# Attention beside the first product by whole tiles of 128 tokens, with another decoding order and another end

## The chip, the cores and the metric

The kernel runs on one core of one Trainium2 chip. The metric is the device time of one execution in microseconds. Three runs of the kernel before took 1620.76, 1622.3 and 1623.78 us; the median is 1622.3.

## The reference

Attention over chunks of 64 tokens (8 batches, 8 heads, 576 tokens, 64 wide), then two dense blocks over 4608 tokens (512 to 2048 to 512), the first with a squared relu, the second with a smooth step:

```python
def _attn_ref(q, k, v):            # all cut into chunks of 64 tokens
    scores = (1 / sqrt(D)) * matmul(q_c, k_c^T)
    scores = scores - max(scores)
    attn = exp(scores); attn = attn / (sum(attn) + 1e-09)
    return matmul(attn, v_c)

x = attn_out.transpose(0, 2, 1, 3).reshape(B * S, H * D)     # 4608 x 512
h = x @ w_in;  x = (maximum(h, 0) ** 2) @ w_out
h = x @ w_in2; g = where(h >= 1, h, where(h <= -1, 0, (h + 1) ** 2 / 4)); out = g @ w_out2
```

The weights arrive as float64 and are decoded on the chip.

## The kernel before, in words

**Stages.** `plain_h` forms x @ w_in in 9 blocks of 512 tokens; it is the first stage, with attention and all the decoding beside it. Three more stages (`form_b`, `form_a`, `form_b` again) form the other three products with seven half-size products each (P1 to P7) in the manner of Strassen; the change touches of these only the last stores.

**Products.** An operand is held as a high and a low part (xh, xl for x; ih, il for w_in), and each product is three matmuls: high by high, low weight by high, high weight by low.

**Slots.** All instructions are written out by hand in the order of a list of slots. Slot 2 (16 j + fi) + c of the first stage is half c of the product for block j and weight piece fi: six matmuls of 512 columns into `ph`. After the second half, ACT takes the relu (`g`), POOL squares it, and SP issues the store to DRAM. `ph` has two banks, so the relu of a piece must be done before the product after the next begins. Slots 0 to 287 are the first stage (SB1 = 288). `at_slot(s, fn)` puts a helper behind the six matmuls of slot s; what was registered first comes first. Each engine, and SP with its DMA issues, works through its own part of this order strictly in sequence; a slot fixes the order, not the time.

**Attention.** A tile is 128 tokens, a unit four heads of a tile (UT = 2 units a tile, 72 units). A unit goes through: `att_a` (four transposes of q and k into psA), `att_ae` (ACT copies them to qkT), `att_b` (psB, the scores, and DVE's maximum m), `att_exp` (ACT, four exponentials with their sums z), `att_n` (DVE adds 1e-9 and takes the reciprocal, POOL scales s), `att_c` (two transposes into psC), `att_ce` (ACT to atT), `att_d` (psD, the product with v), `att_x` (ACT xh, DVE xl). `head(i)` runs this for the first tiles ahead of the loop, one unit a step. In the loop `turn(i)` takes four slots (PER = 4) and holds the parts of four units: slot 0 of a turn psD of the unit three back, psB and its maximum of the unit one back, and xh, xl; slot 1 the exponentials; slot 2 psC, atT and the normalising of the unit behind; slot 3 psA, qkT and the loads of later tiles.

**Decoding of w_in.** `stage_piece` loads a piece (two buffers `ws`), `piece_a` takes its absolute value on ACT and runs three bit operations on DVE (tile `wy`), `piece_b` one more on DVE and then ACT's copy to ih, `piece_c` subtracts on POOL (il). `decode()` runs c, b and a of three neighbouring pieces; six decodes stand in the head (DEC), the others are spread over the first slots (PACE), each ahead of its slot's attention.

**Decoding of the other weights.** 48 units (`unit_a` to `unit_d`: DVE, POOL sums, ACT, DVE, stores) start at slot U0 = 22, one every UPER = 5.1 slots; `stage_unit` of the first two stands three slots ahead.

**The end.** In the last stage P4's tiles of the last token pair are copied by ACT from PSUM, transposed by DVE (`store`) and stored with four DMAs each, all issued by SP.

Of the kernel before, what the change touches and what calls it, by code (L numbers as in the profile page):

```python
# [8 lines left out]
F32 = mybir.dt.float32  # L9
# [22 lines left out]
def chunk_attention_moe_moe2(ctx, tc, q, k, v, w_in1, w_out1, w_in2, w_out2, out):  # L32
# [91 lines left out]
    def wy():  # L124
        n_y[0] += 1
        return rt(4 + n_y[0] % 3, [P, 4 * P], "wy", U32)
# [123 lines left out]
    att = {}  # L250
# [45 lines left out]
    def att_ae(u):  # L296
        qkT = ep.tile([P, 2, NP, P], F32, tag="qkT", name="qkT", bufs=2)
        nc.scalar.activation(out=qkT[:, 0], in_=att[u][:, 0], func=AF.Copy, scale=SCALE)
        nc.scalar.copy(qkT[:, 1], att[u][:, 1])
        att[u] = qkT  # L300

    def att_b(u):

        qkT = att[u]
        pt = pa.tile([P, 2, 512], F32, tag="qk", name="psB")
        for p in range(NP):
# [9 lines left out]
        sc = pt[:, :, 0:2 * CH].rearrange("q e (c k) -> q e c k", c=2)  # L316
        m = ep.tile([P, 2, 2], F32, tag="m", name="m", bufs=3)
        z = ep.tile([P, 2, 2], F32, tag="z", name="z", bufs=3)
        nc.vector.tensor_reduce(out=m, in_=sc, op=ALU.max, axis=AX.X, negate=True)
        att[u] = [sc, m, z]  # L320

    def att_exp(u):
        sc, m, z = att[u]
        s = ep.tile([P, 2, 2, CH], F32, tag="s", name="s", bufs=2)
        for e in range(2):
            for c in range(2):
# [7 lines left out]
        att[u] = [s, z]  # L334

    def att_n(u):
        s, z = att[u]
        nc.vector.tensor_scalar_add(z, z, 1e-9)
        nc.vector.reciprocal(z, z)
        s4 = s.rearrange("q e c k -> q (e c) k")  # L340
        z4 = z.rearrange("q e c -> q (e c)")
        nc.gpsimd.tensor_tensor(out=s4, in0=s4, in1=z4.unsqueeze(2).to_broadcast([P, HU, CH]), op=ALU.mult)

    def att_c(u):
        s, _ = att[u]
        pt = pa.tile([P, 2, NP, CH], F32, tag="t", name="psC", padded_shape=[P, HU, 2, CH], bufs=2)
        for e in range(2):
            nc.tensor.transpose(  # L348
                pt[:, e].rearrange("k p t -> k (p t)"), s[:, e].rearrange("q c k -> q (c k)"), ident
            )  # L350
        att[u] = pt

    def att_ce(u):
        at = ep.tile([P, 2, NP, CH], F32, tag="atT", name="atT", bufs=2)
        nc.scalar.copy(at, att[u])
        att[u] = at

    def att_d(u):

        at = att[u]  # L360
        pt = pa.tile([P, 2, 512], F32, tag="d", name="psD")
        for p in range(NP):
            for c in range(2):
                for e in range(2):
                    nc.tensor.matmul(  # L365
                        pt[rows(e), c, p * CH:(p + 1) * CH],
# [5 lines left out]
        att[u] = pt  # L372

    def att_x(u):
        pt = att.pop(u)
        (xh, xl), a, n = unit_x(u)[0]
        o = pt[:, :, 0:NP * CH].rearrange("d c (p t) -> d p c t", p=NP)
        xh, xl = (x.rearrange("d p (c t) -> d p c t", c=2) for x in (xh, xl))
        nc.scalar.copy(xh, o)
        nc.vector.tensor_tensor(out=xl, in0=o, in1=f(xh), op=ALU.subtract)  # L380
# [16 lines left out]
    RG = tuple(range(7, 13))  # L397
# [167 lines left out]
    def form_b(w, j, prod, kk):  # L565
# [20 lines left out]
        for dp in range(2):  # L586
            c = c_tile(n)
            if key is None:
# [11 lines left out]
    def store(j, dh, th, dp, c):  # L600
# [5 lines left out]
        for a in range(P // G):  # L606
            nc.sync.dma_start(
# [10 lines left out]
    LB, LC, LD, LV = 1, 2, 3, 0  # L618
    PER = 4
    DEC = (1, 2, 4, 6, 8, 10)  # L620
    PACE = 0.78
    U0, UPER = 22, 5.1
# [28 lines left out]
    with tc.manual_schedule():  # L651
# [14 lines left out]
        strokes = []  # L666
        for p in range(NF):
            strokes.append([(piece_a, p), (piece_b, p), (piece_c, p)])
# [14 lines left out]
        def turn(i):  # L683

            res = [[] for _ in range(4)]

            def put(n, fn, u):
                if 0 <= u < NU:
                    res[n].append((fn, (u,)))

            put(0, att_d, i - LD)
            put(0, att_b, i - LB)
            put(0, att_x, i - LD)
            put(1, att_exp, i - LB)
            put(2, att_c, i - LC)
            put(2, att_ce, i - LC)
            put(2, att_n, i - LB)
            put(3, att_a, i)
            put(3, att_ae, i)
            if i >= LV and (i - LV) % UT == 0 and i - LV < NU:  # L700
                res[3].append((load_v, ((i - LV) // UT,)))
            if i % UT == UT - 1 and i // UT + QB < NU // UT:
                res[3].append((load_qk, (i // UT + QB,)))
            return res

# [4 lines left out]
        n0 = tiles_until(0) * UT  # L710
        def head(i):
            def do(fn, u, hi=NU):
                if 0 <= u < hi:
                    fn(u)

            do(att_b, i - LB)
            do(att_x, i - LD - 1)
# [4 lines left out]
            do(att_ae, i)  # L722
            do(att_ce, i - LC)
            if i in DEC:
                decode()
            do(att_n, i - LB)
            if (i - LV) % UT == 0:
                load_v((i - LV) // UT)
            if i % UT == UT - 1:
                load_qk(i // UT + QB)  # L730

        for i in range(n0 + LD):
            head(i)
        att_x(n0 - 1)
        for i in range(n0 + LD, NU + LD):
            g = int((i - n0 - LD) * PER)
            for c, group in enumerate(turn(i)):
                for fn, args in group:
                    at_slot(g + c, fn, *args)

        for j in range(1, NBL):
            assert int((tiles_until(j) * UT - 1 - n0) * PER) < 2 * NF * j, j
        done = int((NU + LD - 1 - n0 - LD) * PER) + 4

# [110 lines left out]
        for s in range(END + 40):  # L855
# [3 lines left out]
            if n_dec[0] < NF + 2 and n_dec[0] < len(DEC) + 1 + PACE * ((s + 2) // 2):  # L859
                decode()  # L860
# [6 lines left out]
        assert not todo and not pe and not wst and n_dec[0] == NF + 2  # L867
# [32 lines left out]
```

## Time and profile before

| | |
|---|---|
| median of three runs | 1622.3 us |
| profiled execution | 1622.09 us, its span 1620.3 us |
| mean granted TensorE clock | 0.994 |
| TensorE busy | 1586.6 us (98%) |
| DVE, ACT, POOL busy | 1089.7, 868.5, 413.3 us (67, 54, 26%) |

The span runs from the first to the last instruction; what the measured time holds beyond it lies around the program. An engine's busy share is over the whole span; stages differ, so the windows further down say more. A wait in brackets is idle time just before that group of instructions, and the name behind the arrow is what ended it.

### The profile page before, as it was taken

How to read it: one execution, taken by the hardware profiler on the slowest of the kernel's cores; microseconds unless marked ns; L12 is line 12 of the kernel's file. 1: busy time of each engine (PE TensorE's matmuls, PEld its weight loads, DVE VectorE, ACT ScalarE, POOL GpSimd, SP SyncE). 2: the span in 40 equal slices, each digit the busy share in tenths (PEclk: the TensorE clock that was granted, in tenths of full speed). 3: DMA queues.
4: the chain of work that ended last, by engine and by line, in shares of the span. 5: the costliest groups of instructions: out<-in, count | busy, mean ns of one | idle time of the engine just before them, and what ended most of it. 6: DMA issues, size and time to landing. Idle time of an engine off the chain costs nothing.

```text
span 1620.3 us, 27342 instructions
## 1 busy us (share of the span) xinstructions
PE 1586.6 (98%) x9504; PEld 1362.6 (84%) x9504; DVE 1089.7 (67%) x1437; ACT 868.5 (54%) x1852; POOL 413.3 (26%) x461
## 2 busy tenths in 40 slices
PE   7889999999999999999999999999999999999998
PEld 5667777777778899999888898898888899998887
DVE  5956666665443376777677666857574787877786
ACT  7656666666553344344444566666665434444442
POOL 2657666665444200000000333333220000000000
PEclk9999999999999999999999999999999999999999
DMA  9769999999996982625378665574679773563723
GB/s 213 204 185 295 291 290 287 293 302 281 277 301 205 318 250 91 216 62 190 110 219 254 210 230 178 190 238 159 240 244 337 248 199 99 129 170 83 207 37 49
DMA packets 442730, 339.47 MB, mean 210 GB/s; under 512 B 214240, under 2 KB 419040, under 8 KB 442592
## 3 DMA queue, kind: packets, MB, share of 16 engines
q1 hardware_dynamic: 442592, 337.73, 69.3%
q8 instruction: 75, 1.23, 0.3%
q14 instruction: 63, 0.52, 0.1%
HBM read 195.04 MB, written 142.61 MB: 208 GB/s over the span
## 4 chain that ended last, share of the span: by engine, by line
PE 87%; DVE 5%; ACT 2%; DMA 2%; issue 2%; POOL 1%; SPq 0%; DVEq 0%; ACTq 0%; POOLq 0%
PE X L451 34%; PE ph L409 23%; PE V L451 17%; PE W L451 8%; PE psA L291 1%; PE psD L365 1%; PE psB L309 1%; DVE ol L441 1%; DVE t L532 1%; PE psC L348 1%; DMA ws<-in_moe_w_in_dram 1%; ACT s L327 1%; DVE wy L115 1%; DVE xr L445 0%; DVE wy L118 0%
## 5 line engine op out<-in xcount | busy, mean ns | idle before, releaser
L451 PE MATMUL X<-oh,w 128*128 128x448 f32 (+1 forms) x1920 | 557.5, 371 | 1.5 <-DVE c L512 1.5
L440 ACT CAST oh<-gr 128x896 fp32r<-128x896 f32 (+1 forms) x280 | 270.0, 964 | 334.1 <-PE X L451 160.5
L441 DVE TENSOR_TENSOR ol<-gr,oh 128x896 fp32r<-128x896 f32 (+1 forms) x280 | 314.5, 1124 | 182.6 <-ACT oh L440 175.3
L451 PEld LDWEIGHTS X<-oh,w 128*128 128x128 f32 x1920 | 360.0, 188 | 43.8 <-DVE c L512 1.9
L451 PE MATMUL X<-ol,w 128*128 128x448 f32 (+1 forms) x960 | 356.4, 371 | 4.2 <-DVE ol L441 4.2
L451 PE MATMUL V<-oh,w 128*128 128x448 f32 (+1 forms) x960 | 278.5, 371 | 0.0
L409 PE MATMUL ph<-xh,ih 128*128 128x512 f32 x576 | 245.3, 426 | 0.0
L409 PE MATMUL ph<-xl,ih 128*128 128x512 f32 x576 | 227.9, 396 | 0.0
L409 PE MATMUL ph<-xh,il 128*128 128x512 f32 x576 | 227.8, 395 | 0.0
L422 POOL TENSOR_TENSOR g<-g 128x512 f32<-128x512 f32 x144 | 171.3, 1189 | 143.6 <-ACT g L421 140.5
L451 PEld LDWEIGHTS X<-ol,w 128*128 128x128 f32 x960 | 180.1, 188 | 26.7 <-DVE ol L441 6.3
L451 PEld LDWEIGHTS V<-oh,w 128*128 128x128 f32 x960 | 180.2, 188 | 20.9
L445 DVE TENSOR_TENSOR gr<-gr,gr 128x896 f32<-128x896 f32 (+1 forms) x160 | 177.9, 1112 | 3.7 <-DMA gr<-g 3.7
L451 PE MATMUL V<-ol,w 128*128 128x448 f32 (+1 forms) x480 | 178.0, 371 | 0.0
L421 ACT ACTIVATE g<-ph 128x512 f32<-128x512 f32 x144 | 86.4, 600 | 134.8 <-PE ph L409 123.3
L451 PE MATMUL W<-oh,w 128*128 128x448 f32 (+1 forms) x480 | 139.4, 371 | 0.0
L409 PEld LDWEIGHTS ph<-xl,ih 128*128 128x128 f32 x576 | 109.3, 190 | 24.7
L409 PEld LDWEIGHTS ph<-xh,ih 128*128 128x128 f32 x576 | 109.4, 190 | 21.6
L409 PEld LDWEIGHTS ph<-xh,il 128*128 128x128 f32 x576 | 110.0, 191 | 16.6
L526 ACT ACTIVATE t<-c,half 128x448 f32<-128x448 f32 (+1 forms) x120 | 81.3, 681 | 70.9 <-DVE c L512 70.8
L441 POOL TENSOR_TENSOR ol<-xr,oh 128x896 fp32r<-128x896 f32 (+1 forms) x10 | 23.7, 2374 | 360.7 <-ACT oh L440 353.0
L532 DVE SCALAR_TENSOR_TENSOR t<-c,t 128x448 f32<-128x448 f32 (+1 forms) x120 | 96.4, 830 | 18.4 <-ACT t L526 18.2
(69 smaller groups left out, 1906.0 us busy)
## 6 DMA issues: line engine op xcount, KB each, us to landing
w<-w SPq DMA_DIRECT2D x168, 256.0 KB, 5.1
gr<-g SPq DMA_DIRECT2D x96, 448.0 KB, 5.2
gr<-g SPq DMA_DIRECT2D x64, 480.0 KB, 4.6
g<-t SPq DMA_DIRECT2D x96, 224.0 KB, 2.7
wu<-in_moe_w_out_dram SPq DMA_DIRECT2D x64, 256.0 KB, 4.6
g<-t SPq DMA_DIRECT2D x64, 240.0 KB, 4.4
w<-wh SPq DMA_DIRECT2D x32, 448.0 KB, 4.1
w<-wl SPq DMA_DIRECT2D x32, 448.0 KB, 5.0
```

The lines of the kernel that those rows point to most:

```text
L115: nc.vector.scalar_tensor_tensor(out=y, in0=w1, scalar=0xC0000000, in1=y, op0=ALU.bitwise_and, op1=ALU.bitwise_or)
L291: nc.tensor.transpose(pt[:, i, p, :], qkn[i][:, h0 + 2 * p:h0 + 2 * p + 2, :].rearrange("p h d -> p (h d)"), ident)
L309: nc.tensor.matmul(pt[rows(p), e, c * CH:(c + 1) * CH], qkT[rows(e), 0, p, rows(c)], qkT[rows(e), 1, p, rows(c)], start=True, stop=True,)
L409: nc.tensor.matmul(ph, win[fi][wi][:, kt * P:(kt + 1) * P], x[:, i, :], start=(kt == 0 and a == 0), stop=(kt == KT - 1 and a == 2),)
L421: nc.scalar.activation(out=g, in_=ph, func=AF.Relu)
L422: nc.gpsimd.tensor_tensor(out=g, in0=g, in1=g, op=ALU.mult)
L440: nc.scalar.copy(hi, raw)
L441: eng.tensor_tensor(out=lo, in0=raw, in1=f(hi), op=ALU.subtract)
L445: eng.tensor_tensor(out=o, in0=x, in1=z, op=ALU.subtract)
L451: nc.tensor.matmul(o, wt_[:, wi, c, :], x[:, i, :], start=first and a == 0, stop=last and a == 2, skip_group_check=True,)
L526: nc.scalar.activation(out=t, in_=h, func=AF.Square, bias=half, scale=0.5)
L532: nc.vector.scalar_tensor_tensor(out=t, in0=h, scalar=1.0, in1=t, op0=ALU.max, op1=ALU.min)
```

## The change

- A tile's two units are taken together in the loop: `tile_a` (eight transposes into two psA tiles), `tile_ae`, `tile_b`, `tile_exp` (once for each half e), `tile_n`, `tile_c`, `tile_ce`, `tile_d`, `tile_x`. A tile takes eight slots (PER = 8), g being the slot of its psB: psA at g - 4, psB, maximum and half of the exponentials at g (with psD and x of the tile before), the other half at g + 1, normalising at g + 4, psC and atT at g + 6, psD and x at g + 8. The first loop tile (4) has its psA, psB and exponentials in the head. qkT, s and atT hold a whole tile; qkT and atT have one buffer, s two.
- Of the decoding, ACT's copy to ih becomes a helper of its own (`piece_h`), run one decode later than `piece_b`; `piece_c` follows one later still; `wy` has four buffers and `g` five instead of six. A decode stands behind its slot's attention. The head holds seven (1, 2, 3, 5, 7, 9, 10), PACE is 0.8.
- U0 = 28 and UPER = 5 for the other weights.
- At the end P4's tiles of the last pair go from PSUM to DVE's transpose without ACT's copy, and of the last pair's first half of tokens (P2 and P4) every second store is issued by ACT.

```diff
-        return rt(4 + n_y[0] % 3, [P, 4 * P], "wy", U32)
+        return rt(4 + n_y[0] % 4, [P, 4 * P], "wy", U32)
...
+    def piece_h(p):
+        y, hi, lo = wst[p]
         nc.scalar.copy(hi, f(y))
...
+    def tile_a(t):
+        att[t, "a"] = []
+        for i in range(2):
+            pt = pa.tile([P, UT, NP, P], F32, tag="t", name="psA", bufs=2)
+            for h in range(0, H, 2):
+                nc.tensor.transpose(
+                    pt[:, h // HU, h // 2 % NP, :], qks[t][i][:, h:h + 2, :].rearrange("p h d -> p (h d)"), ident
+                )
+            att[t, "a"].append(pt)
+
+    def tile_ae(t):
+        q_, k_ = att.pop((t, "a"))
+        qkT = qkT_of(t * UT)
+        nc.scalar.activation(out=qkT[:, :, 0], in_=q_, func=AF.Copy, scale=SCALE)
+        nc.scalar.copy(qkT[:, :, 1], k_)
...
+    def normalize(s, z):
         nc.vector.tensor_scalar_add(z, z, 1e-9)
         nc.vector.reciprocal(z, z)
+        nc.gpsimd.tensor_tensor(out=s, in0=s, in1=z.unsqueeze(3).to_broadcast(list(s.shape)), op=ALU.mult)
...
+    def tile_b(t):
+        pt = pa.tile([P, 2, 512], F32, tag="qk", name="psB")
+        for i in range(UT):
+            scores(pt[:, :, i * 2 * CH:(i + 1) * 2 * CH], qkT_of(t * UT)[:, i])
+        att[t, "b"] = maxima(pt, UT * 2)
+
+    def tile_exp(t, e):
+        exps(s_of(t * UT), *att[t, "b"], (e,), UT * 2)
+
+    def tile_n(t):
+        normalize(s_of(t * UT), att.pop((t, "b"))[2])
...
+    def tile_c(t):
+        att[t, "c"] = pt = pa.tile([P, UT, 2, NP, CH], F32, tag="t", name="psC", bufs=2)
+        for i in range(UT):
+            turned(pt[:, i], s_of(t * UT), i)
+
+    def tile_ce(t):
+        nc.scalar.copy(at_of(t * UT), att.pop((t, "c")))
...
+    def tile_d(t):
+        att[t, "d"] = pt = pa.tile([P, 2, 512], F32, tag="d", name="psD")
+        for i in range(UT):
+            weigh(pt, t * UT + i, i * NP * CH)
+
+    def tile_x(t):
+        pt = att.pop((t, "d"))
+        for i in range(UT):
+            x_parts(pt, t * UT + i, i * NP * CH)
...
-    RG = tuple(range(7, 13))
+    RG = tuple(range(8, 13))
...
+            if key is None and w == 1 and j == NPAIR - 1:
+                store(j, dh, th, dp, o[dp])
+                continue
...
-            nc.sync.dma_start(
+            (nc.scalar if j == NPAIR - 1 and th == 0 and a % 2 else nc.sync).dma_start(
...
-    PER = 4
-    DEC = (1, 2, 4, 6, 8, 10)
-    PACE = 0.78
-    U0, UPER = 22, 5.1
+    PER, PH = 8, 4
+    DEC = (1, 2, 3, 5, 7, 9, 10)
+    PACE = 0.8
+    U0, UPER = 28, 5
...
-            if 0 <= n - 2 < NF:
-                piece_c(n - 2)
-            if 0 <= n - 1 < NF:
-                piece_b(n - 1)
+            for d, fn in ((3, piece_c), (2, piece_h), (1, piece_b)):
+                if 0 <= n - d < NF:
+                    fn(n - d)
...
+            if i == n0:
+                tile_a(T0_)
...
+            if i == n0 + 1:
+                for e in range(2):
+                    tile_exp(T0_, e)
...
+        for t in range(T0_, NTI):
+            g = PER * (t - T0_ - 1) + PH
+            if t > T0_:
+                at_slot(g - 4, tile_a, t)
+                at_slot(g - 4, tile_ae, t)
+                at_slot(g - 4, load_v, t)
+                if t + QB < NTI:
+                    at_slot(g - 4, load_qk, t + QB)
+                at_slot(g, tile_b, t)
+                at_slot(g, tile_x, t - 1)
+                at_slot(g, tile_exp, t, 0)
+                at_slot(g + 1, tile_exp, t, 1)
+                at_slot(g + 4, tile_n, t)
+            at_slot(g + 6, tile_c, t)
+            at_slot(g + 6, tile_ce, t)
+            at_slot(g + PER, tile_d, t)
+        at_slot(g + PER, tile_x, t)
...
-            if n_dec[0] < NF + 2 and n_dec[0] < len(DEC) + 1 + PACE * ((s + 2) // 2):
-                decode()
             i = 0
             while i < len(todo.get(s, ())):
...
             todo.pop(s, None)
+            if n_dec[0] < NF + 3 and n_dec[0] < len(DEC) + 1 + PACE * ((s + 2) // 2):
+                decode()
```

## Rows read from the trace of the kernel before

**Rows 1.** The page, part 4: the chain that ended last, by engine.
```profile
PE 87%; DVE 5%; ACT 2%; DMA 2%; issue 2%; POOL 1%; SPq 0%; DVEq 0%; ACTq 0%; POOLq 0%
```
**Rows 2.** Windows: start:end us, length, busy us (instructions) by engine, PEclk, DMA share, GB/s.
```profile
24.00:40.00 16.00, 14.23 (x174) 10.27 (x173) 11.65 (x29) 14.02 (x64) 5.41 (x7) 1.00 0.98 197
40.00:84.00 44.00, 39.87 (x314) 30.97 (x313) 40.93 (x58) 26.08 (x79) 29.01 (x23) 0.92 0.72 203
52.00:60.00 8.00, 6.96 (x48) 5.51 (x49) 7.56 (x12) 5.31 (x18) 5.70 (x5) 0.57 0.55 171
130.00:494.00 364.00, 364.00 (x3193) 288.68 (x3183) 217.69 (x396) 229.46 (x791) 215.60 (x271) 1.00 0.96 291
```
**Rows 3.** Windows of tile wy alone: length, busy DVE, ACT, POOL, then as above.
```profile
40.00:84.00 44.00, 35.64 (x37) 5.81 (x10) 15.04 (x9) 0.92 0.72 203
24.00:40.00 16.00, 7.55 (x12) 1.81 (x3) 3.05 (x3) 1.00 0.98 197
```
**Rows 4.** Timeline of TensorE, one steady turn: start us, us, instruction [idle before].
```profile
304.42 0.60 PE L291 MATMUL psA<-ident,qkn 128*128 128x128 f32 x4
...
306.02 0.40 PE L409 MATMUL ph<-xl,ih 128*128 128x512 f32 x1
306.34 0.46 PE L365 MATMUL psD<-atT,vt 64*64 64x64 f32 x16
306.62 0.47 PE L309 MATMUL psB<-qkT 64*64 64x64 f32 x16
...
309.88 0.38 PE L348 MATMUL psC<-ident,s 128*128 128x128 f32 x2
...
311.49 0.60 PE L291 MATMUL psA<-ident,qkn 128*128 128x128 f32 x4
```
**Rows 5.** The chain in order of time, products without attention: start us, us, what.
```profile
503.67 47.83 PE ph L409 x210
```
**Rows 6.** Timeline of DVE behind one maximum, first and last of nine instructions.
```profile
285.96 0.42 DVE L319 TENSOR_REDUCE m<-psB 128x4 f32<-128x256 f32 x1 [1.93 <-PE psB L309]
...
291.24 0.92 DVE L196 SCALAR_TENSOR_TENSOR wc<-wa,wy 128x512 f32<-128x512 f32 x1
```
**Rows 7.** Timeline of POOL, one stretch of the steady loop.
```profile
293.02 1.94 POOL L184 TENSOR_TENSOR wc<-wc 128x128 f32<-128x128 f32 x4
295.25 1.04 POOL L422 TENSOR_TENSOR g<-g 128x512 f32<-128x512 f32 x1 [0.29 <-ACT g L421]
296.94 0.63 POOL L342 TENSOR_TENSOR s<-s,z 128x256 f32<-128x256 f32 x1 [0.65 <-DVE z L339]
```
**Rows 8.** Timeline of TensorE in the first turns of the loop.
```profile
41.86 0.46 PE L365 MATMUL psD<-atT,vt 64*64 64x64 f32 x16
...
52.71 0.70 PE L365 MATMUL psD<-atT,vt 64*64 64x64 f32 x16 [3.67 <-ACT atT L355]
...
85.65 0.46 PE L365 MATMUL psD<-atT,vt 64*64 64x64 f32 x16 [1.09 <-ACT atT L355]
...
98.97 0.73 PE L309 MATMUL psB<-qkT 64*64 64x64 f32 x16 [5.01 <-ACT qkT L299]
...
114.81 0.46 PE L365 MATMUL psD<-atT,vt 64*64 64x64 f32 x16
```
**Rows 9.** Timeline of ACT ahead of two of these waits.
```profile
51.21 0.62 ACT L150 CAST ih<-wy 128x512 fp32r<-128x512 f32 x1 [2.23 <-DVE wy L147]
...
97.22 0.67 ACT L111 ACTIVATE wa<-wu 128x512 f32<-128x512 f32 x1 [4.49 <-DMA wu<-in_moe_w_out_dram]
```
**Rows 10.** Timeline of ACT at the end.
```profile
1612.47 1.20 ACT L589 COPY c<-X 128x480 f32<-128x480 f32 x2 [6.33 <-PE X L451]
```
**Rows 11.** Timeline of DVE at the end.
```profile
1613.07 1.32 DVE L604 STREAM_TRANSPOSE ct<-c 128x480 f32<-128x480 f32 x2 [5.73 <-ACT c L589]
```
**Rows 12.** Timeline of SP's queue at the end.
```profile
1613.77 4.09 SPq L607 DMA_DIRECT2D out_dram<-ct  x8
```
**Rows 13.** Window of the last transfers, columns as in rows 2.
```profile
1614.60:1619.00 4.40, 0.00 (x0) 0.00 (x0) 0.00 (x0) 0.00 (x0) 0.00 (x0) 0.60 0.71 112
```

More of the change, by code (lines that the diff above doesn't have):

```diff
@@ L246, in load_w, with of_tile, qkT_of, s_of @@
         wt[m, a, prod] = t
-    att = {}
+    att, ttile = {}, {}
+    def of_tile(name, u, shape, bufs=1):
+        if (name, u // UT) not in ttile:
+            ttile[name, u // UT] = ep.tile(shape, F32, tag=name, name=name, bufs=bufs)
+        return ttile[name, u // UT]
+    def qkT_of(u):
+        return of_tile("qkT", u, [P, UT, 2, NP, P])
+    def s_of(u):
+        return of_tile("s", u, [P, 2, UT * 2, CH], SBUFS)
+    def at_of(u):
+        return of_tile("atT", u, [P, UT, 2, NP, CH])
     def rows(par):
@@ L296, in att_ae, with scores @@
     def att_ae(u):
-        qkT = ep.tile([P, 2, NP, P], F32, tag="qkT", name="qkT", bufs=2)
+        qkT = qkT_of(u)[:, u % UT]
         nc.scalar.activation(out=qkT[:, 0], in_=att[u][:, 0], func=AF.Copy, scale=SCALE)
         nc.scalar.copy(qkT[:, 1], att[u][:, 1])
-        att[u] = qkT
+    def tile_a(t):
[12 more added lines that the diff above has]
+        nc.scalar.copy(qkT[:, :, 1], k_)
     def att_b(u):
-        qkT = att[u]
         pt = pa.tile([P, 2, 512], F32, tag="qk", name="psB")
+        scores(pt[:, :, 0:2 * CH], qkT_of(u)[:, u % UT])
+        att[u] = maxima(pt, 2)
+    def scores(pt, qkT):
         for p in range(NP):
@@ L315, in att_b, with maxima, exps @@
                     )
-        sc = pt[:, :, 0:2 * CH].rearrange("q e (c k) -> q e c k", c=2)
-        m = ep.tile([P, 2, 2], F32, tag="m", name="m", bufs=3)
-        z = ep.tile([P, 2, 2], F32, tag="z", name="z", bufs=3)
+    def maxima(pt, n):
+        sc = pt[:, :, 0:n * CH].rearrange("q e (c k) -> q e c k", c=n)
+        m = ep.tile([P, 2, n], F32, tag="m", name="m", bufs=3, padded_shape=[P, 2, UT * 2])
+        z = ep.tile([P, 2, n], F32, tag="z", name="z", bufs=3, padded_shape=[P, 2, UT * 2])
         nc.vector.tensor_reduce(out=m, in_=sc, op=ALU.max, axis=AX.X, negate=True)
[L320 to L326, printed above, removed]
+        return [sc, m, z]
+    def exps(s, sc, m, z, es, n):
+        for e in es:
+            for c in range(n):
                 nc.scalar.activation(
@@ L347, in att_c, with att_n, turned @@
+    def att_n(u):
+        normalize(*att[u])
+    def turned(pt, s, n):
         for e in range(2):
             nc.tensor.transpose(
-                pt[:, e].rearrange("k p t -> k (p t)"), s[:, e].rearrange("q c k -> q (c k)"), ident
+                pt[:, e].rearrange("k p t -> k (p t)"), s[:, e, 2 * n:2 * n + 2].rearrange("q c k -> q (c k)"), ident
             )
+    def att_c(u):
+        pt = pa.tile([P, 2, NP, CH], F32, tag="t", name="psC", padded_shape=[P, HU, 2, CH], bufs=2)
+        turned(pt, s_of(u), u % UT)
@@ L351, in att_c @@
         att[u] = pt
     def att_ce(u):
-        at = ep.tile([P, 2, NP, CH], F32, tag="atT", name="atT", bufs=2)
-        nc.scalar.copy(at, att[u])
-        att[u] = at
+        nc.scalar.copy(at_of(u)[:, u % UT], att[u])
+    def tile_c(t):
[4 more added lines that the diff above has]
+        nc.scalar.copy(at_of(t * UT), att.pop((t, "c")))
     def att_d(u):
-        at = att[u]
@@ L681, in decode @@
                     stage_piece(n + 2)
[L683 to L704, printed above, removed]
         def tiles_until(j):
@@ L726, in head @@
             do(att_n, i - LB)
-            if (i - LV) % UT == 0:
-                load_v((i - LV) // UT)
-            if i % UT == UT - 1:
+            if i <= n0 and i % UT == 0:
+                load_v(i // UT)
+            if i < n0 and i % UT == UT - 1:
                 load_qk(i // UT + QB)
+            elif i == n0:
+                load_qk(T0_ + QB)
         for i in range(n0 + LD):
             head(i)
+        tile_n(T0_)
         att_x(n0 - 1)
[L735 to L739, printed above, removed]
+        NTI = NT // P
+        for t in range(T0_, NTI):
[15 more added lines that the diff above has]
+        at_slot(g + PER, tile_x, t)
         for j in range(1, NBL):
-            assert int((tiles_until(j) * UT - 1 - n0) * PER) < 2 * NF * j, j
-        done = int((NU + LD - 1 - n0 - LD) * PER) + 4
+            assert PER * (tiles_until(j) - 1 - T0_) + PH + 2 < 2 * NF * j, j
+        done = g + PER + 2
         units = [(m, a, b) for m in range(3) for a in range(8) for b in range(2)]
@@ L866, in chunk_attention_moe_moe2 @@
             todo.pop(s, None)
-        assert not todo and not pe and not wst and n_dec[0] == NF + 2
+            if n_dec[0] < NF + 3 and n_dec[0] < len(DEC) + 1 + PACE * ((s + 2) // 2):
+                decode()
+        assert not todo and not pe and not wst and n_dec[0] == NF + 3
 _INS = ["q", "k", "v", "moe_w_in", "moe_w_out", "moe2_w_in", "moe2_w_out"]
```

49 lines of the change are left out of this document (26 added, 23 removed).

## The prediction

> **What bounds the kernel now.** I read the chain of waits first, then stage windows, then one turn of the loop on TensorE, then the places where it waits. The chain is TensorE for 87% [rows 1]: time is gained only where TensorE issues fewer or cheaper pieces, or where it waits. The windows show three stages that matter [rows 2]. From 130 to 494 us TensorE is busy all of the time, DVE 60%, ACT 63%, POOL 59%: nothing but TensorE's own order counts there. From 40 to 84 us it waits, and DVE is the full engine, 40.93 of 44 us; 35.64 of these belong to decoding w_in (tile `wy`, 37 instructions, so 3.85 us for a decode of four) [rows 3]. After 551 us, where the first product ends [rows 5], the change touches nothing but the last stores.
>
> One turn of the steady loop (one unit, which is four heads of a tile; four slots, 24 products) takes 311.49 - 304.42 = 7.07 us, from psA to psA [rows 4]. A product alone takes 47.83 / 210 = 0.228 us [rows 5], 24 take 5.47, so attention costs 1.60 us a unit. Between psC at 309.88 and psA at 311.49 lie 1.61 us with six products (1.37): psC's two transposes cost 0.24. From psA at 304.42 to the end of the sixth product after it (306.02 + 0.23) are 1.83 us: four transposes cost 0.46. Two equations give 0.108 us a transpose and 0.03 for each switch. From 306.25 to psC at 309.88 are 3.63 us with twelve products (2.73): psD and psB together cost 0.90. Sixteen psD instructions last from 306.34 to 306.62, 0.28 us, 0.0175 each; sixteen psB at that pace are another 0.28; the rest, 0.34, is paid once a group (0.09 before psD, the remainder on the way back to products).
>
> **Part 1, whole tiles.** The same matmuls are issued, but a tile's two units share one group: one psD+psB group in eight slots instead of two, one psA, one psC. Saved in eight slots: 0.34 + 0.03 + 0.03 = 0.40 us. The loop has 31 such tiles (5 to 35): 12.3 us. The lower bound is that the 0.34 grows with the length of the group and only the switches of the transposes are saved: 31 x 0.06 = 1.9. The upper one is that the 0.09 before psD goes from the remaining group too, since psA now lies four slots ahead of psB and not one: 12.3 + 2.8 = 15.1. I take 12.3, because the inner pace is read from the row itself.
> The Trainium skill speaks against this part ("TensorE: Matmul & The Clock Gate", the passage on 56 and 53.3 ns): small matmuls start no closer than about 25 ns. By that, 64 of them in a row would need 1.6 us plus the 0.34, 0.14 more than the 1.80 that the two groups take now, and this part would lose 31 x 0.08 = 2.5 us instead of gaining 12.3. Sixteen in 0.28 us [rows 4] are closer than that, so I keep the row; the case has its place among the rivals, as C.
> ACT, DVE and POOL issue fewer, larger instructions (two qkT copies a tile instead of four, one maximum, one sum and reciprocal); they are not the bound here and this gains nothing. The transposes' evacuation now has four slots, so ACT is no longer late for psB.
>
> **A tighter place that the change makes.** Normalising a tile stands in slot g+4, its psC in g+6 (g: the slot of psB). Before, four slots lay between the two, now two. From psB's end to psC TensorE has six slots of products and one psA: 0.2 + 6 x 1.37 + 0.9 = 9.3 us. In that time DVE must do the maximum, two xl and the decoding of w_out or w_in2 that is queued between, and POOL its squares and sums before it may scale s. Where a unit's three DVE parts fall right behind the maximum, a row of such a stretch goes from 285.96 to 292.16, 6.2 us with nine instructions [rows 6]; with the wider maximum and the second xl, but without z, 6.5. On POOL then come four sums (1.94), a square (1.04) and the scaling of twice the width (2 x 0.63) [rows 7]: 6.5 + 1.94 + 1.04 + 1.26 = 10.7, late by 1.4 us; with DVE at its less disturbed pace about 1 us less. Units come every 5 slots, tiles every 8, so this meets one tile in five, another one in five misses by at most 0.6, and only the 32 units that have sums count: three tiles and four. I take 4 us lost (0 to 7). Behind a late psC wait the next products, and everything else runs on.
>
> **Part 2, the decoding order and the start of the loop.** psD of slot 0 starts at 41.86, psD of slot 32 at 114.81: 72.95 us for eight turns, 16.4 more than 8 x 7.07 [rows 8]. Where it goes: 3.67 us before the psD at 52.71 (ACT's copy to atT stands behind the copy of ih, which waits 2.23 us for DVE's wy [rows 9]), and then the granted clock is 0.57 in 52 to 60 us [rows 2], near the lower of its two levels (1.2 of 2.4 GHz), which I put at 2 us; 1.09 before the psD at 85.65; and 5.01 before psB at 98.97, because ACT's wa stands 4.49 us before the first wu load [rows 9] with qkT behind it; that load is slot 19's, held up in SP's queue behind stores that wait for POOL. After this longer wait I put another 2 us at the lower level.
> The change puts the copy of ih one decode later than the product it needs, puts decoding behind the attention of its slot, does seven decodes instead of six in the head, ends piece_a in slot 16 instead of 20, and moves the first wu loads from slots 19 and 20 to 25 and 26 on SP's queue, behind slot 24's v, q and k loads. What goes: the wait at 98.97 with the lower clock behind it and the one at 85.65 (together about 8 us), since by slot 25 POOL has done its last il and DVE its last wy. What does not: DVE stays full from 40 us on. Three decodes in slots 0 to 2 (3 x 3.85 = 11.6 us) stand ahead of slot 4's maximum while TensorE needs 7 to 8 us to get there; ACT then holds psB's exponentials and behind them the relu that frees a bank. I expect 3 to 4 us of waiting about slot 6 to 8 in place of the 3.67, and 1 to 2 twice more (psC in slots 10 and 18). So I take 8 us gained here (-2 if the first wait grows and the wu wait only moves; 14 if nearly all 16.4 go).
> The seventh decode in the head costs 7.55 / 3 = 2.5 us of DVE [rows 3], which has 4.35 of 16 free there; ACT, busy 14.02 of 16 [rows 2], gets its two more operations but loses unit 10's qkT and unit 8's atT. Cost 0 (-1 to +2, in the 8 us above). With UPER 5 the last unit ends two slots later; the loads after it have twelve slots: 0. Five g buffers instead of six still cycle in 5 x 3.5 = 17.7 us: 0.
>
> **Part 3, the end.** The last two tiles lose ACT's copies, 1.20 us for two [rows 10], of which 0.6 stands on the path (the first of them; DVE's transposes wait on it [rows 11]). Eight issues on SP take 4.09 us [rows 12]; four go to ACT. If issues are the limit, the last starts 2 us earlier, 2.6 in all; if the DMA engines are, busy 0.71 in that stretch [rows 13], the 4.4 us of transfers shrink to 3.1 at best, and with the 0.6 it is 1.9; if the two queues share what limits them, 0.6. I take 2.0. The Trainium skill ("DMA: Bandwidth & Descriptors", Issuing engines are not separate DMA queues) says that issuing from two engines saves only the sequencer's time, usually small beside the transfer; here the row makes it most of the tail. P2's stores put four issues (2 us) before ACT's last cast; ACT is 2% of the chain [rows 1], so I cost it at 0 (to -2, if that cast has no lead at all).
>
> **Sum.** 12.3 - 4 + 8 + 2.0 = 18.3 us off the profiled execution's own 1622.09 (span 1620.3 and 1.8 around it): 1603.8. The median of three, 1622.3, is 0.2 above that execution: 1604.
>
> **Rivals.**
> A: the start gains nothing. DVE at 40.93 of 44 us speaks for it: waits move but stay, and the wu load is late again. 1622.3 - 12.3 + 4 - 2 = 1612.
> B: everything goes well: all but 2 us of the early waits go, psC is never late. 1622.3 - 12.3 - 14 - 2.6 = 1593.4. For it: ACT's slack of four slots; against: DVE's load.
> C: grouping does not pay. Either the pace of small matmuls in a long row falls to where two groups cost the same, or the DMA engines, at 0.96 in 130 to 494 us [rows 2], cannot go faster and hold the pace. For it: that share; against: nothing on TensorE waits for a DMA there. 1622.3 - 0 + 4 - 8 - 2 = 1616 (1619 if a group gets dearer by 0.1 a tile).
> D, slower: normalising comes too late in every tile, not in one of five. Each psC then waits 1.4 us, and 31 x 1.4 = 43 stand against 22.3 gained: 1643. It decides from 0.7 us a tile on. For it: a POOL chain that ends at 10.7 against 9.3; against: in three of five phases the decoding is not in that stretch, and the last sixteen units have no sums.
> E: the change does nothing that shows: pieces cancel.
>
> **Chances.** Forecast 0.48, A 0.15, B 0.15, C 0.10, D 0.10, E 0.02. About 0.2% (3 us) is what a measurement of this kernel can tell from no change. Faster 0.48 + 0.15 + 0.15 + 0.06 of C = 0.84; same 0.04 of C + 0.02 = 0.06; slower 0.10. Range 1593 to 1619: it leaves out D, the slow end of C, half of B's fast end.
>
> **What would show it.** Right: two psA x8 apart by eight slots in 13.8 us in place of 14.15, a group of psD x32 and psB x32 that lasts about 1.1 us from start to start of the next product but for 0.2; psC with waits of about 1 us on POOL in a few tiles only; psD or psB waits near 50 to 60 us but none of 5 us near 95; about 3 us from the last matmul to the last store issued instead of 5. Wrong: an unchanged period, or psC waiting in every tile, or a wait on wu that has only moved to slot 28.

## The result and the profile after

The changed kernel takes 1632.4 us (median of six, 1629.7 to 1638.5) against 1621.6 (six); ratio 1.0073, interval 1.0055 to 1.0091. It is 11 us slower; 18 us faster was predicted. The execution profiled is the longest of the six, 1638.5 us with a span of 1636.7. In it the first product ends at 513.95 + 47.83 = 561.78 us:
```profile
513.95 47.83 PE ph L487 x210
```
That is 10.3 us behind [rows 5]; the medians differ by 10.7. The rest of what this execution lost lies in a stage that the change does not touch: TensorE waits 4.33 us there instead of 1.51, and the granted clock is 0.62 from 1275 to 1284 us (1.00 in that stage before):
```profile
1277.26 1.17 PE L529 MATMUL X<-oh,w 128*128 128x480 f32 x2 [4.33 <-DVE c L590]
```
Four of the other five executions are 5 to 9 us shorter, so most did not lose this; it is left out below.

The page's chain by engine shows TensorE at 74% instead of 87% [rows 1]:
```profile
PE 74%; DVE 6%; DMA 5%; ACT 5%; POOL 4%; issue 4%; SPq 1%; POOLq 0%; DVEq 0%; ACTq 0%
```
The windows of the kernel after, columns as in [rows 2]:
```profile
24.00:40.00 16.00, 11.44 (x150) 7.89 (x150) 7.89 (x21) 10.83 (x51) 4.85 (x6) 1.00 0.97 192
40.00:84.00 44.00, 36.31 (x285) 29.01 (x286) 39.45 (x49) 27.50 (x82) 25.72 (x19) 0.96 0.71 188
130.00:494.00 364.00, 347.34 (x3098) 280.71 (x3097) 214.34 (x314) 220.99 (x696) 217.52 (x246) 1.00 0.95 278
```
The stage from 130 to 494 us, where TensorE never waited [rows 2], now has 16.7 us without it. TensorE's list of waits from 130 to 562 us (us in total, times, longest) has one entry that matters, and psC's weight load, which the list for all engines has apart, waits for the same s. In the list for all engines from 43 to 562 us stands an entry on ACT that the experiments come back to:
```profile
PE psC L401 <- POOL s L376: 16.3, 13, 2.0
```
```profile
ACT xh L447 <- DVE xl L448: 44.2, 32, 5.1
```
From 403 us on, where no unit with sums is left, the turns are undisturbed (timeline of TensorE, kernel after):
```profile
403.57 0.69 PE L432 MATMUL psD<-atT,vt 64*64 64x64 f32 x32
404.08 0.75 PE L347 MATMUL psB<-qkT 64*64 64x64 f32 x32
404.76 0.50 PE L487 MATMUL ph<-xh,ih 128*128 128x512 f32 x1
...
410.36 1.03 PE L326 MATMUL psA<-ident,qkn 128*128 128x128 f32 x8
...
413.97 0.60 PE L401 MATMUL psC<-ident,s 128*128 128x128 f32 x4
...
417.27 0.69 PE L432 MATMUL psD<-atT,vt 64*64 64x64 f32 x32
```
417.27 - 403.57 = 13.70 us for eight slots, where two turns took 14.14 [rows 4]. So the saving of part 1 is there, 0.44 us a tile. From 130 to 403 us only about one turn in five is undisturbed; the others last 14.0 to 17.4 us. One of the long ones, by engine (TensorE, then ACT, DVE, POOL; wa, wy, wc, wh and wl are tiles of the decoding of the other weights, and its sums write wc):
```profile
298.15 0.75 PE L347 MATMUL psB<-qkT 64*64 64x64 f32 x32
...
310.08 0.66 PE L401 MATMUL psC<-ident,s 128*128 128x128 f32 x4 [1.81 <-POOL s L376]
```
```profile
298.42 0.37 ACT L447 CAST xh<-psD 128x256 fp32r<-128x256 f32 x1 [1.47 <-PE psD L432]
300.01 0.38 ACT L447 CAST xh<-psD 128x256 fp32r<-128x256 f32 x1 [1.22 <-DVE xl L448]
...
303.93 0.72 ACT L111 ACTIVATE wa<-wu 128x512 f32<-128x512 f32 x1
```
```profile
298.95 0.69 DVE L359 TENSOR_REDUCE m<-psB 128x8 f32<-128x512 f32 x1 [3.00 <-PE psB L347]
299.56 0.41 DVE L448 TENSOR_TENSOR xl<-psD,xh 128x256 fp32r<-128x256 f32 x1
...
301.21 0.69 DVE L115 SCALAR_TENSOR_TENSOR wy<-wu,wy 128x512 uint32<-128x512 uint32 x1
...
304.68 0.69 DVE L199 SCALAR_TENSOR_TENSOR wc<-wa,wy 128x512 f32<-128x512 f32 x1 [1.05 <-ACT wa L111]
305.29 1.01 DVE L374 TENSOR_SCALAR z<-z 128x8 f32<-128x8 f32 x1
...
307.01 0.84 DVE L115 SCALAR_TENSOR_TENSOR wy<-wu,wy 128x512 uint32<-128x512 uint32 x1
```
```profile
296.82 1.95 POOL L187 TENSOR_TENSOR wc<-wc 128x128 f32<-128x128 f32 x4
...
306.24 2.79 POOL L187 TENSOR_TENSOR wc<-wc 128x128 f32<-128x128 f32 x4
308.99 1.04 POOL L376 TENSOR_TENSOR s<-s,z 128x512 f32<-128x512 f32 x1
```
Read from bottom to top: POOL scales s behind four sums of a unit; these stand behind DVE's wc, which waits for ACT's wa; wa stands behind the eight exponentials (with a copy wh and a relu between them); these stand behind the second xh; and that waits 1.22 us for DVE's first xl, itself queued behind the maximum. The chain goes through all three engines. The four sums, too, take 2.79 us here and 1.95 a little earlier, where DVE's bit operations (L115) do not run beside them; more on this below.

### The profile page after: what moved, and what is told of

It reads as the page before. It is cut to its first block, busy times and chain, and to the rows that moved or that the text cites. A ratio compares the mean times of both kernels' runs of the same rounds, so it can differ in the third digit from the quotient of the medians.

```text
span 1636.7 us, 26929 instructions
## 1 busy us (share of the span) xinstructions
PE 1579.4 (96%) x9504; PEld 1363.0 (83%) x9504; DVE 1090.7 (67%) x1341; ACT 862.3 (53%) x1754; POOL 414.0 (25%) x429
## 4 chain that ended last, share of the span: by engine, by line
PE 74%; DVE 6%; DMA 5%; ACT 5%; POOL 4%; issue 4%; SPq 1%; POOLq 0%; DVEq 0%; ACTq 0%
PE X L529 33%; PE V L529 17%; PE ph L487 13%; PE W L529 8%; ACT s L365 2%; POOL s L376 1%; POOL g L500 1%; PE psC L401 1%; DMA g<-g 1%; PE psD L432 1%; PE psB L347 1%; DVE ol L519 1%; DVE t L610 1%; POOL wc L187 1%; DVE wy L115 1%
## 5 line engine op out<-in xcount | busy, mean ns | idle before, releaser
L487 PE MATMUL ph<-xh,ih 128*128 128x512 f32 x576 | 236.6, 411 | 5.8 <-ACT g L499 5.8
```

What stands on the lines that cost most here:

```text
L487: nc.tensor.matmul(ph, win[fi][wi][:, kt * P:(kt + 1) * P], x[:, i, :], start=(kt == 0 and a == 0), stop=(kt == KT - 1 and a == 2),)
```

## The experiments

Where psC waits, three things stand in dispute: the place of the normalising in the queues, the chain ahead of it, or the short distance from psB to psC. "First stage" is the start of its last product (561.4 us in the kernel after, 551.1 before), "idle" what TensorE lacks of 364 us from 130 to 494.

**Normalising earlier.**
```diff
-                at_slot(g + 4, tile_n, t)
+                at_slot(g + 2, tile_n, t)
```


> The changed kernel with one edit: a tile's normalising (reciprocal on DVE, scaling of s on POOL) is queued in slot g+2 instead of g+4, so it stands ahead of the decoding and the squares of slots g+2 and g+3. Theory 1 (its place in the queues makes psC late): the waits of psC on POOL's s in stage 1, 33.3 us over 35 entries in the changed kernel, fall below 10 us, and the time is 1611 us or less (1632 - 21). Rival 2 (the chain ahead of it is late: ACT's second copy xh, the exponentials, POOL's sums): the sums end no earlier, DVE now waits for them with the decoding behind it; psC still waits 15 us or more in all and the time stays at 1626 to 1636. Rival 3 (the early wait for the sums holds DVE up): slower than 1636.


1624.9 us, ratio to before 1.0025 (1.0014 to 1.0035); first stage 554.1, idle 6.7. Between the forecasts. From 130 us on psC no longer waits on s. But DVE now waits for the exponentials with the decoding queued behind it, and ACT's wh later for POOL's sums (list of waits, 43 to 562 us; 9.7 us in 8 entries and 32.4 in 24 in the kernel after):
```profile
ACT wh L212 <- POOL wc L187: 51.9, 24, 3.3
DVE z L374 <- ACT s L365: 44.4, 31, 2.5
```
At the start, where DVE is full, this costs: the psD after 120 us starts at 124.50 instead of 120.24, 4.3 of the gain given back. Theory 1 holds for the steady stage; at the start rival 3's mechanism is seen, though not its time.

**Both copies xh first.**
```diff
+        todo_x = []
         for i in range(UT):
-            x_parts(pt, t * UT + i, i * NP * CH)
...
+            nc.scalar.copy(xh, src)
+            todo_x.append((xl, src, xh))
+        for xl, src, xh in todo_x:
+            nc.vector.tensor_tensor(out=xl, in0=src, in1=f(xh), op=ALU.subtract)
```


> The changed kernel with one edit: a tile's two copies xh are issued on ACT ahead of DVE's two subtractions xl. In the changed kernel ACT's second xh waits for DVE's first xl in each tile (44.2 us over 32 entries of the wait list), and the eight exponentials stand behind it. Rival 2 of the experiment with the earlier normalising (the chain ahead of normalising is late): ACT is 1.2 us earlier in each tile, psC's waits on s fall by 0.8 to 1.2 us in some 15 tiles, the time falls by 12 to 18 us, to 1614 to 1620. Theory 1 (place of the normalising in the queues decides): ACT's wait goes, psC's waits stay within 5 us of 33, the time stays at 1629 to 1635.


1620.3 us, ratio 0.9995 (0.9983 to 1.0007): 12 us less than the kernel after, the low end of rival 2's gain. First stage 549.1, idle 9.8. ACT's wait for xl has left the list, and TensorE's waits from 130 to 494 us are (after: 16.1 in 12 entries)
```profile
PE psC L401 <- POOL s L376: 10.0, 11, 1.4
```
So the chain ahead of normalising is a cause: its head start comes through to s, about 0.5 us in each late tile. It is not the whole 1.22 us, because the exponentials now wait for DVE's maximum (list of waits for all engines, 43 to 562 us):
```profile
ACT s L365 <- DVE m L359: 23.9, 30, 3.5
```

**psC one slot later.**
```diff
-            at_slot(g + 6, tile_c, t)
-            at_slot(g + 6, tile_ce, t)
+            at_slot(g + 7, tile_c, t)
+            at_slot(g + 7, tile_ce, t)
```


> The changed kernel with one edit: psC and the copy to atT one slot later, g+7 instead of g+6, with psD where it was at g+8. A slot of six products takes 1.37 us. Both theories of why s is late give the same for psC: each wait shrinks by 1.37 us, so of the repeating waits 0, 0.25, 2.0, 0.84, 2.1 us only 0.63 and 0.73 stay, 6 us of 22. What is in dispute is what then becomes late: ACT's copy to atT (0.9 us) and psD have one slot left instead of two. If that is enough where ACT is not behind, the time falls by 12 to 16 us to 1617 to 1620; if psD takes the wait over (ACT with relu and wa ahead of the copy), psD waits about as long as psC did and the time stays at 1628 to 1634.


1618.5 us, ratio 0.9983 (0.9971 to 0.9995); first stage 546.9, idle 9.5. The slot takes 12 us off psC's wait, and a part of it comes back where the rival put it, at psD behind ACT's copy to atT (same list):
```profile
PE psD L432 <- ACT atT L419: 5.8, 5, 2.0
PE psC L401 <- POOL s L376: 3.7, 7, 0.6
```

**Both edits.** The two diffs above together.


> The changed kernel with two edits together: both copies xh ahead of the two subtractions xl, and psC with its copy to atT one slot later. Alone, the first left waits of psC of 1.43, 0.31 and 1.49 us in five tiles (302.84, 316.9, 332.16), the second left 0.65 and 0.70 before psC and 1.37 before a psD whose atT ACT copied late. Theory (two separate causes, the chain on ACT and the slots left, whose gains add): psC's waits of 1.4 us vanish under the extra slot of 1.37 us, ACT is 1.2 us earlier for atT, the repeating waits fall under 0.5 us per five tiles, and the first stage ends 8 to 12 us before that of the kernel with the later psC alone: 1607 to 1611. Rival (one cause removed twice, what remains is ACT's own load): psD's wait of 1.37 us stays, and the time stays at 1615 to 1619.


1610.0 us, ratio 0.9922 (0.9902 to 0.9943). First stage 539.1: 12.0 before the kernel before, 22.3 before the kernel after. From 130 to 494 us psC has no wait left (TensorE's list, then the window):
```profile
PE psD L432 <- ACT atT L419: 2.2, 4, 1.0
```
```profile
130.00:494.00 364.00, 361.58 (x3272) 296.28 (x3271) 216.76 (x330) 230.11 (x726) 226.28 (x250) 1.00 1.00 293
```
The gains nearly add up: by first stages 12.3 and 14.5 us alone, 22.3 together. The time is within the theory's range; the first stage ends 7.8 us before that of the later psC alone, just short of the 8 to 12. With psC's waits gone the change is worth 12 us.

**Whole tiles with the old decoding order.** The buffers of wy and g, DEC, PACE, U0, UPER, piece_h and the place of decode() as before the change:
```diff
-    DEC = (1, 2, 3, 5, 7, 9, 10)
-    PACE = 0.8
-    U0, UPER = 28, 5
+    DEC = (1, 2, 4, 6, 8, 10)
+    PACE = 0.78
+    U0, UPER = 22, 5.1
...
```


> The changed kernel with the decoding order and the start of the kernel before (three wy buffers, the copy of ih beside its product, six decodes in the head, piece_u from slot 22 at every 5.1 slots); whole tiles and the new end stay. Theory (whole tiles bring the late psC whatever the decoding order; the new order and its start are worth 1 to 3 us): psC still waits 15 to 25 us on s in the first stage and the time is 1632 to 1636. Rival 1 (the new order is what makes normalising late): psC's waits fall under 8 us, the time is 1612 to 1618. Rival 2 (the new order costs by itself, by its later first product): 1627 to 1631 with psC's waits unchanged.


1645.8 us, ratio 1.0137 (1.0120 to 1.0154), slower than any forecast. The late psC is there whatever the order (18.5 us in 12 entries from 130 to 494 us), as the theory had it, but it put the order's worth, 1 to 3 us, far too low: the first stage ends at 574.9 us, 13.5 later than in the kernel after. TensorE's waits are in the start:
```profile
56.70 1.14 PE L429 MATMUL psD<-atT,vt 64*64 64x64 f32 x32 [4.49 <-ACT atT L416]
...
89.43 0.66 PE L398 MATMUL psC<-ident,s 128*128 128x128 f32 x4 [3.58 <-POOL s L373]
...
106.54 0.66 PE L398 MATMUL psC<-ident,s 128*128 128x128 f32 x4 [1.64 <-POOL s L373]
...
121.39 0.80 PE L484 MATMUL ph<-xh,ih 128*128 128x512 f32 x1 [5.91 <-ACT g L496]
```
The last is for the relu, which stands on ACT behind wa, the second xh (1.94 us for xl) and four exponentials; wa waited for a load of wu, as in [rows 9]:
```profile
116.42 0.67 ACT L111 ACTIVATE wa<-wu 128x512 f32<-128x512 f32 x1 [6.56 <-DMA wu<-in_moe_w_out_dram]
```

**The new decoding order alone,** on the kernel before: the reverse of that diff.


> The kernel before with the decoding order and the start of the changed one (copy of ih one decode later, seven decodes in the head, decoding behind the attention of its slot, four wy buffers, piece_u from slot 28 at every 5 slots), attention by units of half a tile as before. The prediction put this part at 8 us gained (-2 to 14): 1614. What the changed kernel's slots show (ahead by 3.6 us at slot 28, by 0.9 at slot 44, of which whole tiles have brought some 1 to 2) makes it 0 to 3 us: 1619 to 1622. Rival (the seventh decode and the moved order hold up units' short chains more than those of whole tiles): slower than 1624.


1617.5 us, ratio 0.9966 (0.9954 to 0.9978): 5.5 us gained. First stage 544.8, 6.3 earlier. This lies between the prediction's 8 and the 0 to 3 read afterwards from the changed kernel, where other waits cover it. The wait of 5.01 us near 99 us [rows 8] is gone; a psD at 114.50 waits 1.78 us for atT instead. The first product starts at 39.62 us (39.01 before), so the seventh decode in the head costs 0.6 us.

**The new end alone,** on the kernel before.
```diff
+            if key is None and w == 1 and j == NPAIR - 1:
+                store(j, dh, th, dp, o[dp])
+                continue
...
-            nc.sync.dma_start(
+            (nc.scalar if j == NPAIR - 1 and th == 0 and a % 2 else nc.sync).dma_start(
```


> The kernel before with the new end alone (last two tiles stored from the second product's result without ACT's copies, four of the last eight stores issued by ACT). In the changed kernel the stretch from the last matmul's end to the end of the span is 0.9 us shorter than before (7.2 to 6.3). Theory: here too it shrinks by 0.9, from ACT's copy (0.6) and the issues, whose gain the later landing takes back. Rival (the 2.0 of the prediction, hidden in the changed kernel by where its execution fell): 2.0.


From the last matmul's end to the end of the span 6.26 us, before 7.20: 0.94, the theory; this is one execution. Its time, 1621.7, tells nothing at this size.

**The head, first try:** tile 4's exponentials a step later, behind x of units 6 and 7, on the kernel after. x(6) itself stays where it was; x(7) leaves its old place.
```diff
-            if i == n0 + 1:
+            if i == n0 + 2:
+                att_x(n0 - 1)
                 for e in range(2):
                     tile_exp(T0_, e)
```


> The changed kernel with one edit in the head: x of unit 6 and then the eight exponentials of tile 4 move from the last two steps to one step later, so that x(6) does not stand behind the exponentials on ACT. In the changed kernel psD of unit 7 waits 3.39 us for x(6) and the first product starts at 43.40 us instead of 39.01. Theory (that wait is the head's whole loss): the first product starts at 39.5 to 40.5, and the end of the first stage moves by the same 3 to 4 us, the time to 1628 to 1629.5. Rival (DVE, full at 40 us, gives it back): the first product starts early, but the wait for the relu at 64 us grows by as much, and the time stays at 1631 to 1634.


1636.4 us, ratio 1.0088 (1.0071 to 1.0105). The first product comes at 43.63: psD of unit 7 still waits 2.96 us, since DVE's xl(6) stands behind four operations of a decode too. The edit missed its aim; ACT's xh(6) comes 1.6 us earlier, and nothing follows from it.

**The head, second try:** x(6) ahead of both.
```diff
             if i == n0 + 1:
+                att_x(n0 - 2)
                 for e in range(2):
                     tile_exp(T0_, e)
```
(and x(6) leaves its old place)


> The changed kernel with the edit of the head alone (x of unit 6 a step earlier, ahead of tile 4's exponentials and a decode). Theory (the late x(6) is the head's loss of 4.4 us against the kernel before): first product at 40 to 41 us instead of 43.4, first stage 2 to 3 us shorter, 1629 to 1630.5. Rival (DVE is full there and gives it back): 1631.5 to 1633.5 with a longer wait for the relu about 64 us.


1636.3 us, ratio 1.0089 (1.0059 to 1.0119). The first product comes at 41.2 instead of 43.4, and it is given back, as the rival had it: the psD that starts at 74.51 in the kernel after starts at 74.84 here (TensorE's waits; in the kernel after one of 4.79 at 64.11):
```profile
47.31 0.50 PE L487 MATMUL ph<-xl,ih 128*128 128x512 f32 x1 [0.62 <-DVE xl L448]
...
58.69 0.50 PE L487 MATMUL ph<-xh,ih 128*128 128x512 f32 x1 [2.80 <-ACT g L499]
64.43 0.50 PE L487 MATMUL ph<-xh,ih 128*128 128x512 f32 x1 [1.53 <-ACT g L499]
71.47 0.66 PE L401 MATMUL psC<-ident,s 128*128 128x128 f32 x4 [1.80 <-POOL s L376]
```
That it is slower than the kernel after is not clear: its four executions (1632.6, 1633.1, 1639.4, 1641.9) overlap those of the kernel after, and the one profiled is the longest, with a wait of 4.0 us and a clock of 0.62 in the later stage, as there. The first stage of this execution is 4.4 us longer, which the trace does not put down to the head: three of its turns with a late psC last 17.4 us in place of 15.8, against one in the kernel after. In those the clock falls. The same stretch behind the same wait of 1.9 us, first in the kernel after, then here (columns as in [rows 2]):
```profile
194.00:198.00 4.00, 4.00 (x77) 3.18 (x76) 1.65 (x3) 0.97 (x2) 2.87 (x6) 1.00 1.24 277
```
```profile
194.00:198.00 4.00, 4.00 (x17) 2.94 (x19) 1.31 (x1) 0.99 (x2) 1.71 (x2) 0.66 1.15 232
```
Products follow each other there at first in 0.43 us instead of 0.23, the lower of the clock's two levels (1.2 of 2.4 GHz). Two such turns more are 3 us. Why the clock falls behind one wait of 1.9 us and not behind the next stays open.

**On the faster version: the head, and earlier wu loads.** The first adds the head's second try to both edits; the second also moves the first two loads of wu.
```diff
-                at_slot(g - 3 + n, stage_unit, *u)
+                at_slot(g - 5 - 2 * n, stage_unit, *u)
```


> The kernel with both copies xh first and the later psC, and in the head one more edit: x of unit 6 (ACT's xh and DVE's xl) is issued in the step before, ahead of tile 4's eight exponentials and of a decode. In the kernel with tile 4's exponentials moved back, unit 7's psD still waited 3.2 us, then for DVE's xl behind four operations of the decode, so two things stood ahead of x(6), not one. Theory (x(6) behind both): the psD of unit 7 starts within 1.5 us of that of unit 6, the first product starts at 40 to 41 us instead of 43.5, and the first stage ends 2 to 3 us earlier: 1607 to 1608. Rival (DVE, full until 65 us, decides when the early products may run): the first product is early, the waits at 57 and 64 us grow by as much, 1609.5 to 1611.

> The kernel with both copies xh first, the later psC and x of unit 6 earlier, and one more edit: the first two loads of wu stand in slots 23 and 26 instead of 25 and 31, ahead of the v, q and k loads of slot 28 and of two or three stores of g on SP's queue. Theory (the wait at 117 to 118 us, 3.1 us before a psD whose atT stands on ACT behind wa, is that of wa for the second wu load): ACT's wait of 4.5 us for wu falls under 1 us, psD's wait falls under 1 us, 1.5 to 3 us less than without the edit. Rival (the load waits for its buffer, or for the stores ahead of it, wherever it is queued): no change within 1 us.


With the head 1613.8 us, ratio 0.9949 (0.9931 to 0.9967); first product at 40.96, first stage 541.9: the rival, and worse than it. The psD near 58 us waits 5.9 us instead of 3.6 without the edit, which gives the head's gain back. Of the 2.7 us by which this first stage ends later than without the edit, some 1.5 are the clock, 0.72 from 134 to 140 us (1.00 without). With the loads as well 1609.6, 0.9928 (0.9910 to 0.9945), first stage 536.9: the waits of 2.4 and 2.0 before the psD at 118 and 134 us become 0 and 0.6, the theory. The time falls by 4.2 us, more than forecast; the same 1.5 us of the clock are in that, since with the loads it stays at 1.00 behind the psD that waited at 134 us.

**The loads without the head.**


> The kernel with both copies xh first and the later psC, and the earlier wu loads, without the edit of the head. In the kernel with that edit the first product came 2.6 us earlier and the psD at 57 to 59 us waited 2.3 us longer, with another 1 us before a product at 47 us; the wait of 3.1 us before the psD at 117 us went with the earlier wu loads. Theory (the head's edit gives nothing, the loads give 2 to 3 us): the first stage ends at 535 to 537 us, 1605.5 to 1608. Rival (the two edits work only together): 1609 or more.


1607.9 us, ratio 0.9911 (0.9897 to 0.9924), first stage 535.6: the fastest version by median, 14 us below the kernel before and 24 below the changed one. By time it is not clear of the version without the earlier loads (0.9922); by first stage it is 3.5 us ahead. TensorE's waits from 43 to 562 us:
```profile
PE psD L432 <- ACT atT L419: 4.7, 5, 2.3
PE psD L432 <- DVE xl L448: 3.4, 1, 3.4
PE ph L494 <- ACT g L506: 1.4, 2, 1.1
PE psC L401 <- POOL s L376: 0.8, 2, 0.4
```

## Why the prediction was wrong

**The step that failed** is "a tighter place that the change makes", taken at 4 us (0 to 7). The sum over the trace of the kernel after is some 22 us (what lies between the last product's start and psC's, beyond 0.23 us): in five tiles psC waits 0, 0.25, 2.0, 0.84 and 2.1 us, and so on until 403 us. The mechanism and its place were the prediction's, the rival D's as well; D's condition, 0.7 us a tile, was passed while units have sums (1.04 us on average). Four things were left out of the working:
- The first xl makes ACT's second xh wait, 1.22 us, with the exponentials, relu and wa behind it. I costed DVE, POOL and TensorE, and called ACT no bound. Undoing this coupling gave 12 us. It is not the only cause: psC a slot later, with the coupling left in, gave 14.
- DVE's wc waits for ACT's wa (1.05 us), so the delay on ACT reaches the sums. I had a full DVE queue, not two queues that wait on one another. z took 1.01 us (0.17 in the kernel with normalising earlier).
- The sums were costed at the 1.94 us of [rows 7]. From 130 to 410 us that is what all 29 unbroken groups of four take in the kernel before (1.93 to 1.97), none of them beside DVE's bit operations on two inputs (L115, L118). In the kernel after 17 of the 26 unbroken groups do run beside these and take 2.79 to 2.92; the other nine do not and take 1.95. That is 0.85 us on the way to s. No experiment moves the one without the other, so this is read from the traces, not shown by a run.
- From "tiles every eight, units every five slots" I took that one tile in five is met and one more nearly. Four in five were, two of them by 0.84 us or less; a unit's instructions are spread over three engines and several slots.

**Part 1** was right: 0.44 us a tile, predicted 0.40. (Its two equations give 0.11 us a transpose and 0.02 a switch, not 0.108 and 0.03, so they say 0.38; in the sum that is 0.6 us.) The 25 ns floor of rival C ("TensorE: Matmul & The Clock Gate" of the Trainium skill) does not show here: 32 psD from 403.57 to 404.08 are 0.016 us each.

**Part 2**, 8 us, is 5.5 by time and 6.3 by first stage in units of half a tile, and 13.5 by first stage with whole tiles. It is right in sign, and the size by itself is near. The cost of 0 for the seventh decode in the head holds too (0.6 us). What the working had no term for is tile 4's psA, psB and exponentials in the head: with the old decoding order the first product already comes at 42.13, and in the changed kernel at 43.40 instead of 39.01, because psD of unit 7 waits for x(6). The expected wait about slots 6 to 8 is there too (TensorE, kernel after):
```profile
42.77 0.71 PE L432 MATMUL psD<-atT,vt 64*64 64x64 f32 x16 [3.39 <-DVE xl L448]
...
64.11 0.50 PE L487 MATMUL ph<-xh,ih 128*128 128x512 f32 x1 [4.79 <-ACT g L499]
```
The experiments show that the head's 2 to 3 us come back at the second wait when they are saved at the first. DVE, busy 39.45 of 44 us from 40 to 84 us, is the likely reason; no run relieves it.
The wait on wu only moved (psD at 120.24 waited 1.90 us for atT, behind wa, which stood 4.72 us before its load); this stood among the signs of a wrong prediction, and loading earlier cured it. The prediction also had the slots of the second wu load wrong: in the kernels it stands in slot 25 before and 31 after, not 20 and 26, and in the kernel after it is this load that comes late.

**The end**, 2.0, is 0.94. Issues on two queues, and transposes without ACT's copy:
```profile
1630.52 2.47 ACTq L689 DMA_DIRECT2D out_dram<-ct  x4
```
The last issue ends 2.6 us after the last matmul (1630.43) instead of 4.8 (1613.10 and [rows 12]), 2.2 us gained; but from there to the span's end are 3.7 us instead of 2.4, so 1.3 are given back by the transfers. Of the prediction's three bounds the one for shared limits, 0.6, was the nearest. The rule of the Trainium skill that I set aside ("DMA: Bandwidth & Descriptors", Issuing engines are not separate DMA queues), that issuing from several engines saves only the time to issue, agrees with these rows. What the copy and the queues are worth singly was not tried.

**The sum again**, by first stages. Against 551.1, whole tiles with no late psC and the new order give 539.1, that is 12.0 us, and 535.6 or 15.5 us with the earlier loads, which the change did not have; with the end's 0.94, 13 to 16.4. Parts 1 and 2 had been put at 20.3. By themselves they come near it (31 x 0.44 = 13.6 and 6.3), but together they lose some 8 us to the start: the first product 4.5 us later, and waits of 3.6 and 2.95 us before the psD at 56.93 and 117.38, in the version with both edits. So the prediction's 18.3 was some 5 us above the idea with psC's waits cured, and the change as it stood paid 22 us of such waits.

## What to carry to other kernels

When a change halves the slots between a producer and its consumer, follow the chain over every engine in one timeline, with each queue's order, and count which phases meet it over a whole period, rather than adding up the fullest queue. When two units' results are put side by side in one PSUM tile, look at who reads the halves: issue one engine's reads of both before the other's. Take an instruction's time from a row where the same things run beside it as in the new order. Before taking a wait away at a start, look at which engine is full over the whole start: here the gain was given back.

## What the runs showed of the hardware

In the kernel after, ACT's second xh waits for DVE's first xl, though they read different halves of psD and write different tiles: 44.2 us in 32 entries of the list of waits, none with both xh first. The two halves lie side by side in the same tile, on the same partitions. The Trainium skill ("PSUM — Partial Sum Buffer", PSUM bank collisions raise a hardware error) says that two engines may not access one bank within the same 32 partitions at the same time, two reads included, and that the program has to keep them apart; the waits agree with that, and no run here tries it without them.

POOL's sums and DVE's bit operations on two inputs take longer side by side: 2.79 to 2.92 us instead of 1.95 for four sums, 0.83 instead of 0.69 for one such bit operation, wherever they meet in the kernel after from 130 to 410 us. A third surprise, told above, is that equal waits of 1.9 us are followed by a granted clock of 1.00 in one execution and of 0.66 in another.
